# Sliding attention with a token-mixing MLP behind it: the first k heads loaded as fp32 by SyncE, the first GpSimd load held back, mixing by token halves, and a new order

## The chip, the cores and the metric

The kernel runs on 1 core of one Trainium2 chip. The metric is the device time of one execution, in microseconds (us). Engines are called as in the profile: PE is TensorE (its matmuls; PEld its weight loads), ACT is ScalarE, DVE is VectorE, POOL is GpSimd, SP is SyncE. SP does no arithmetic here: it issues DMAs (transfers), as POOL does beside some small work of its own. PE writes into PSUM, eight banks that the kernel uses as four pairs; only ACT and DVE carry results out of PSUM.

## The reference

Eight batches, eight heads, 576 tokens, 64 columns per head. Attention looks back over a window of 128 tokens with a penalty linear in the distance; its output, heads side by side, is a 576 x 512 matrix per batch, which a small MLP then mixes over the tokens.

```python
scores = scale * np.matmul(q, k.transpose(0, 1, 3, 2))
mask = (rel >= 0) & (rel < window)
scores = np.where(mask, scores + bias[None], -1000000000.0)
attn = softmax(scores)
x = np.matmul(attn, v)              # heads side by side: (B, S, 512)

wq, wk = x @ w_q, x @ w_k           # 64 columns each
W_tok = scale * np.einsum('bsd,btd->bst', wq, wk)
mixed = np.einsum('bst,btd->bsd', W_tok, x)
out = np.maximum(mixed, 0.0) @ w_out
```

The softmax lines and the reshaping are shortened here. The mixing is computed as wq times (wk transposed times x), so no 576 x 576 matrix is formed for it.

## The kernel before

The whole program is one unrolled list of small steps. Each step has a name, runs on one engine, and is a handful of instructions. The text ORDER at the head of the file is the schedule: a list of words `name:engine:bank`, made beforehand by a search, and every engine works through its own words strictly in that order. Nothing is reordered on the chip; a step whose input is late holds up all that stands behind it on its engine.

The steps of batch b, by name:

- Lq, Lk, Lv b.n: loads of q, k, v, issued by POOL, which cast fp32 to fp16 on the way. For b below 4, Lq b.u and Lk b.u bring heads 4u to 4u+3 (into tiles natw). Lt are the last 64 tokens (natt). Lwq, Lwk, Lwo are the weights. A load waits until an earlier load has landed, so that few are under way at a time (AHEAD in `load`).
- FQ0 and FQ1: q's heads 0 to 3 of batch 0 come another way. SP loads two heads each as fp32 into spare output tiles (osb), and CQ0 and CQ1 cast them on ACT or DVE into natw (`add_first`, cast in line 230 or 232).
- TW (or TN from batch 4 on, TT for the last 64 tokens): transposes of q and k on PE; ETW, ETN, ETT: their copies from PSUM into qkT.
- QK b.g.u: scores of key group g for four heads; EXP b.g.u: the exponential on ACT into pt; MUL b.g.u: times a table (bias, or biasl for the last group) on DVE, which also zeroes what lies outside the window. 64 of each.
- PV b.t: attention times v, with the row sum; X b.t: division by it on DVE (lines 654 and 655).
- XT, EXT: transposes of x and their copies. WQ b.0 and b.1 (256 tokens each) and b.2 (64 tokens), EWQ: the projection with w_q. WK, EWK: that with w_k. G, EG: wk transposed times x.
- MX b.j: the mixing matmul. For j = 0 and 1 it makes two of the four blocks of 128 columns for tokens 0 to 511, so it needs both EWQ b.0 and EWQ b.1; j = 2 is for the last 64 tokens. RM: the ReLU from PSUM into rm, one tile per block of 128 columns.
- OUT b.s: the output matmul for 128 tokens, four matmuls that add up over the four blocks of rm, so it needs RM b.0 to b.3. EO: its copy out of PSUM. DO: the store, issued by SP or POOL.

What is prepared at the start: iota (POOL), dist, mask (the table's distances, far and wm, on DVE), bias0 and bias1 (eight exponentials of wm on ACT, line 303), biasl (DVE), and constant fills: ones, zeros, zerop, pads. A word like `TW0.0.0:P:00:14` also asks for 14 matmuls on constant data (tile fill) ahead of the step, which keep PE at work while it has nothing to do.

Of the kernel before, what the change touches and what calls it, by code (L numbers as in the profile page):

```python
# [13 lines left out]
P = 128  # L14
# [13 lines left out]
TOK = 4  # L28
PTW = 1088
# [8 lines left out]
FQ1:S ones0:V FQ0:S Lk0.0:G pads:V iota:G Lk0.1:G dist:V Lt0.0:G idh:V perm:V Lq0.1:G mask:V  # L38
Lt0.2:G ones2:V bias0:A Lt0.3:G zerop:V Lt0.1:G CQ1:V CQ0:A Lk1.1:G bias1:A TW0.0.0:P:00:14
Lv0.1:G TW0.0.1:P:01 ETW0.0.0:A biasl1:V Lq1.1:G ETW0.0.1:A biasl0:V Lv0.0:G QK0.0.0:P:1:5  # L40
QK0.2.0:P:2 EXP0.0.0:A ones4:G TW0.1:P:0:2 EXP0.2.0:A MUL0.0.0:V Lk1.0:G QK0.1.0:P:3
ETW0.1.0:V ETW0.1.1:A Lq1.0:G EXP0.1.0:A zeros:V QK0.1.1:P:0 QK0.0.1:P:1 ones3:V QK0.2.1:P:2
EXP0.1.1:A TT0:P:3 MUL0.2.0:V MUL0.1.0:V EXP0.2.1:A Lv0.2:G ETT0:V MUL0.1.1:V EXP0.0.1:A
QK0.3.0:P:0:3 QK0.3.1:P:2 Lv0.3:G EXP0.3.1:A MUL0.0.1:V Lwq:G TW1.1:P:1:2 EXP0.3.0:A Lv0.4:G
MUL0.3.1:V Lq2.1:G MUL0.2.1:V ETT1:A PV0.0:P:2 ETW1.1.1:A PV0.1:P:0 MUL0.3.0:V Lk2.1:G
ETW1.1.0:A X0.0:V ones1:G QK1.0.1:P:3:2 QK1.1.1:P:1 EXP1.0.1:A X0.1:V Lq2.0:G TW1.0:P:2:2
EXP1.1.1:A MUL1.0.1:V Lwk:G Lk2.0:G PV0.2:P:0 ETW1.0.1:A MUL1.1.1:V QK1.2.1:P:3 ETW1.0.0:A
Lv1.0:G X0.2:V PV0.3:P:1 EXP1.2.1:A QK1.0.0:P:2 Lv1.1:G wqq:V PV0.4:P:0 X0.3:V EXP1.0.0:A
QK1.2.0:P:3 Lv1.2:G X0.4:V EXP1.2.0:A XT0.0:P:1 QK1.3.0:P:2 MUL1.2.1:V XT0.1:P:0 EXT0.0:A
Lv1.3:G TW2.1:P:3 EXT0.1:V EXP1.3.0:A MUL1.0.0:V Lt1.2:G QK1.3.1:P:1 ETW2.1.1:A XT0.2:P:00  # L50
QK1.1.0:P:2 MUL1.2.0:V Lv1.4:G EXP1.3.1:A WQ0.1:P:01 EXT0.2:V WQ0.0:P:31 MUL1.3.0:V Lq3.0:G
WK0:P:00 EXP1.1.0:A EWQ0.1:V MUL1.3.1:V Lt1.3:G TW2.0:P:1 ETW2.1.0:A EWK0:V EWQ0.0:A Lk3.0:G
MUL1.1.0:V WQ0.2:P:01 PV1.0:P:2 ETW2.0.0:A QK2.0.1:P:3 EWQ0.2:V ETW2.0.1:A Lt1.0:G X1.0:V
PV1.1:P:0 EXP2.0.1:A QK2.0.0:P:1 Lt1.1:G X1.1:V PV1.2:P:2 EXP2.0.0:A QK2.2.0:P:3 Lwo.2:G
# [89 lines left out]
def kernel(  # L144
# [214 lines left out]


    loads = {}
    under, gate = [], []
    tw, tt, qkd, pvd = {}, {}, {}, {}

    def load(name, occ, serve, deps, emit, eng="POOL"):
# [23 lines left out]
    def add_first(i):  # L389
# [7 lines left out]
        def cast(o):  # L397
            cp(o.eng, natw_s[0][0][0][:, 2 * i:2 * i + 2, :], first)
# [531 lines left out]
```

## Time and profile before

| what | value |
|---|---|
| time, median of 3 runs | 138.32 us (138.3 to 139.66) |
| the profiled execution: its time | 138.74 us |
| its span (first to last instruction) | 137.0 us |
| PE busy | 125.1 us, 91% |
| ACT busy | 115.0 us, 84% |
| DVE busy | 114.0 us, 83% |
| POOL busy | 100.1 us, 73% |
| DMA traffic | 24.86 MB, mean 181 GB/s |

The profiled execution took 138.74 us, of which 137.0 us lie between its first and last instruction and 1.74 us around them. A line of the timeline gives the start, the duration, the engine, the line in the kernel, the operation and its tiles, and in square brackets how long the engine stood idle before it and which engine it waited for. The chain of waits is followed back from the last instruction, at each step to what released it. PE's busy time counts a matmul until its result is written, and matmuls overlap, so PE can be called busy and still have room.

### The profile page before, as it was taken

To read this page: it belongs to the slowest core of one execution; us is meant where nothing else is said; L and a number is where in the kernel's file an instruction comes from. 1 tells how busy PE (TensorE), PEld (TensorE's weight loads), DVE (VectorE), ACT (ScalarE), POOL (GpSimd) and SP (SyncE) were. 2 spreads that over 40 slices of the span, in tenths; PEclk is the share of its full clock that TensorE was granted. 3 is DMA by queue.
4 is the path that set the end of the run, shared out by engine and by line. 5 is a ranking of instruction groups with operands and counts; after the bars stand their busy time and mean duration, and the time that the engine had idled before them with its cause. 6 is when DMAs were issued, how large, how long until landed. Compare 5 with 4: busy or idle time off the path is not lost.

```text
span 137.0 us, 5557 instructions
## 1 busy us (share of the span) xinstructions
PE 125.1 (91%) x2366; PEld 82.0 (60%) x2366; DVE 114.0 (83%) x257; ACT 115.0 (84%) x190; POOL 100.1 (73%) x145
## 2 busy tenths in 40 slices
PE   6895799899999999999999999999998799999950
PEld 2344467686694766775676656666487665765410
DVE  6636898998899999999999999989999699983430
ACT  3687989999899899899999999889997699655720
POOL 6996999798999999999999999976880002340120
PEclk9999999999999999999999999999999999999996
DMA  4999999999999999999999999999999200899992
GB/s 129 152 157 177 186 171 197 179 160 179 190 164 166 156 155 156 153 149 148 141 135 149 143 142 149 284 164 242 285 359 150 20 0 5 330 319 361 359 313 84
DMA packets 92855, 24.86 MB, mean 181 GB/s; under 512 B 80256, under 2 KB 89344, under 8 KB 92832
## 3 DMA queue, kind: packets, MB, share of 16 engines
q0 software_dynamic: 89376, 18.88, 149.0%
q1 hardware_dynamic: 3456, 5.64, 12.0%
q8 instruction: 18, 0.29, 0.8%
q14 instruction: 5, 0.04, 0.1%
HBM read 29.62 MB, written 9.44 MB: 285 GB/s over the span
## 4 chain that ended last, share of the span: by engine, by line
PE 62%; issue 11%; DVE 10%; ACT 5%; DMA 5%; POOL 4%; POOLq 0%; DVEq 0%; ACTq 0%
PE pair L215 51%; PE pair L218 11%; DMA natw<-in_q_dram 5%; DVE x L655 4%; ACT pt L609 3%; POOL out_dram L224 2%; DVE pt L616 2%; DVE xtl L655 2%; DVE inv L654 1%; POOL natw L221 1%; ACT qkT L236 1%; DVE qkT L499 1%; POOL natt L221 1%; DVE wqq_sb L344 0%; ACT natw L230 0%
## 5 line engine op out<-in xcount | busy, mean ns | idle before, releaser
L609 ACT ACTIVATE pt<-pair 128x1024 f16<-128x1024 f32 x64 | 63.7, 1037 | 4.7 <-PE pair L215 4.3
L221 POOL DMA_DIRECT2D vt<-in_v_dram x40 | 35.6, 927 | 3.3 <-DMA natw<-in_k_dram 2.3
L616 DVE TENSOR_TENSOR pt<-pt,bias 128x1024 f16<-128x1024 f16 x48 | 32.1, 684 | 2.5 <-ACT pt L609 2.1
L215 PE MATMUL pair<-wout_sb,rm 128*128 128x512 f16 x128 | 32.0, 380 | 0.1
L224 POOL DMA_DIRECT2D out_dram<-natw x17 | 10.0, 594 | 22.5 <-DVE natw L232 18.9
L215 PE MATMUL pair<-qkT 64*128 64x256 f16 (+3 forms) x352 | 23.7, 243 | 2.5 <-issue 1.1
L215 PEld LDWEIGHTS <-pt 128*128 128x128 f16 x576 | 20.3, 97 | 5.8 <-issue 3.2
L215 PE MATMUL pair<-vt,pt 128*128 128x65 f16 x576 | 23.4, 193 | 0.1
L221 POOL DMA_DIRECT2D natw<-in_k_dram x24 | 22.1, 938 | 1.4 <-POOLq L914 0.8
L655 DVE TENSOR_TENSOR x<-pair,inv 128x512 f16<-128x512 f32 x32 | 22.1, 691 | 1.1
L221 POOL DMA_DIRECT2D natw<-in_q_dram x23 | 21.4, 938 | 0.0
L215 PEld LDWEIGHTS <-rm 128*128 128x128 f16 x128 | 10.6, 97 | 12.4 <-issue 2.8
L215 PEld LDWEIGHTS <-qkT 64*128 64x128 f16 x352 | 11.3, 94 | 10.4 <-issue 5.5
L230 ACT COPY natw<-pair 128x512 f32<-128x512 f32 x23 | 13.8, 609 | 2.7 <-PE pair L215 2.4
L218 PEld LDWEIGHTS <-natw 128*64 128x64 f16 (+1 forms) x512 | 12.7, 102 | 4.2 <-issue 1.5
L215 PE MATMUL pair<-fill 128*128 128x512 f16 x30 | 9.3, 446 | 2.0 <-DVE fill L346 1.2
L755 ACT ACTIVATE rm<-pair 128x512 f16<-128x512 f32 x19 | 11.0, 617 | 0.0
L616 DVE TENSOR_TENSOR pt<-pt,biasl 128x1024 f16<-128x1024 f16 x16 | 10.8, 682 | 0.2 <-ACT pt L609 0.2
L218 PE MATMUL pair<-permh,natw 128*64 128x128 f16 x256 | 8.7, 221 | 1.4 <-DMA natw<-in_q_dram 0.8
L654 DVE RECIPROCAL inv<-pair 128x8 f32<-128x8 f32 (+1 forms) x40 | 8.1, 202 | 1.1 <-PE pair L215 0.8
L215 PE MATMUL pair<-xT,wqq_sb 128*128 128x256 f16 x64 | 8.8, 273 | 0.0
L757 DVE TENSOR_SCALAR rm<-pair 128x512 f16<-128x512 f32 x13 | 8.6, 683 | 0.1
(78 smaller groups left out, 177.7 us busy)
## 6 DMA issues: line engine op xcount, KB each, us to landing
vt<-in_v_dram POOLq DMA_DIRECT2D x32, 128.0 KB, 6.1
out_dram<-natw SPq DMA_DIRECT2D x15, 256.0 KB, 4.4
out_dram<-natw POOLq DMA_DIRECT2D x13, 256.0 KB, 4.8
natw<-in_k_dram POOLq DMA_DIRECT2D x8, 256.0 KB, 6.3
natw<-in_k_dram POOLq DMA_DIRECT2D x16, 128.0 KB, 5.0
natw<-in_q_dram POOLq DMA_DIRECT2D x16, 128.0 KB, 5.6
natw<-in_q_dram POOLq DMA_DIRECT2D x7, 256.0 KB, 6.6
osb<-in_q_dram SPq DMA_DIRECT2D x2, 256.0 KB, 2.9
```

The lines of the kernel that those rows point to most:

```text
L215: hold(nc.tensor.matmul(*a, **k))
L218: hold(nc.tensor.transpose(*a))
L221: hold(nc.gpsimd.dma_start(**k))
L224: i = (nc.gpsimd if eng == "POOL" else nc.sync).dma_start(**k)
L230: hold(nc.scalar.copy(out_ap, in_ap))
L236: hold(nc.scalar.copy(out_ap.bitcast(FP32), in_ap.bitcast(FP32)))
L609: nc.scalar.activation(out=pt[:, 0:1024], in_=two(s.bank).rearrange("p e c -> p (e c)"), func=AF.Exp, scale=SCALE)
L616: nc.vector.tensor_tensor(out=pt[:, 0:1024], in0=pt[:, 0:1024], in1=bt, op=ALU.mult)
L654: nc.vector.reciprocal(out=inv[r], in_=pxv[r, :, :, 64])
L655: nc.vector.tensor_tensor(out=x[r].rearrange("p (g h d) -> p g h d", g=2, h=4), in0=pxv[r, :, :, 0:64], in1=inv[r].unsqueeze(3).broadcast_ ...
L755: hold(nc.scalar.activation(out=out_ap, in_=in_ap, func=AF.Relu, scale=WSCALE))
L757: hold(nc.vector.tensor_scalar(out=out_ap, in0=in_ap, scalar1=0.0, scalar2=WSCALE, op0=ALU.max, op1=ALU.mult))
```

## The change

Four edits go together.

First, k's heads 0 to 3 of batch 0 are no longer loaded by POOL with a cast (Lk0.0 is gone). SP loads them as fp32, two heads at a time, as FK0 and FK1, and CK0 and CK1 cast them on chip. SP thus issues four loads at the start, in the order FK1, FQ1, FQ0, FK0. The first transposes of heads 0, 1 and of heads 2, 3 (TW0.0.0 and TW0.0.1) each need one q cast and one k cast.

Second, POOL's first load waits until SP's first load has landed.

Third, MX b.0 and b.1 are no longer split by column blocks but by tokens: MX b.j makes all four blocks for tokens 256j to 256j+255, and needs EWQ b.j alone. It is four matmuls of 256 columns in place of two of 512. RM b.2r+j carries two column blocks of that token half, and OUT b.s needs the two RMs of its own half in place of all four.

Fourth, some of the planned durations are changed, and ORDER is solved anew, so nearly every step stands elsewhere.

```diff
-    rm_s = [[sb(f"rm{i}{c}", [P, DM], F16) for c in range(4)] for i in range(2)]
+    rm_s = [[sb(f"rm{i}{n}", [P, 4, 256], F16) for n in range(2)] for i in range(2)]
...
             emit(o)
             n = len(under)
             late = 0.0
+            if not n:
+
+                tc.add_manual_dep(held[0], firsts[0][0].name, LANDED, reason="behind the first load of all")
...
-    def add_first(i):
-        first = osb_s[-1 - i].rearrange("p (h c) -> p h c", h=2)
+    def add_first(j, i):
+        first = (osb_end if i + j == 2 else osb_s[-1 - i - 2 * j]).rearrange("p (h c) -> p h c", h=2)
+        nm = "QK"[j]
 
         def em(o):
-            nc.sync.dma_start(out=first, in_=q[0, 2 * i:2 * i + 2, 0:512, :].rearrange("h (p t) d -> p h (t d)", t=4))
+            hold(nc.sync.dma_start(
+                out=first,
+                in_=(q, k)[j][0, 2 * i:2 * i + 2, 0:512, :].rearrange("h (p t) d -> p h (t d)", t=4)))
+            firsts.append(o.insts or list(held))
...
-            ts = [add(f"TW0.0.{a}", pe(0.46), [loads[0, 0, 0, a], loads[0, 1, 0], perm],
+            ts = [add(f"TW0.0.{a}", pe(0.46), [loads[0, 0, 0, a], loads[0, 1, 0, a], perm],
...
-                for r in range(2):
-                    h = slice(64 * r, 64 * r + 64)
-                    mm(pm[:, r, :], g[h, P * j:P * j + P], w[h, 0:512], start=True, stop=True)
+                for d in range(2):
+                    for r in range(2):
+                        h = slice(64 * r, 64 * r + 64)
+                        mm(pm[:, r, 256 * d:256 * d + 256], g[h, P * d:P * d + P],
+                           w[h, 256 * j:256 * j + 256], start=True, stop=True)
...
-        need = [ewq[b, 0], ewq[b, 1]] if j < 2 else [ewq[b, 2]]
-        t = add(f"MX{b}.{j}", pe(0.226, 0.1) if j < 2 else pe(0.06, 0.12), [egs[b], *need], em, banks=2, mode=1)
+        t = add(f"MX{b}.{j}", pe(0.23, 0.1) if j < 2 else pe(0.06, 0.12), [egs[b], ewq[b, j]], em, banks=2, mode=1)
...
-                lt = rm_s[b % 2][db][:, P * st:P * st + P] if st < 4 else rmt_s[(b // 2) % 2][:, db, :]
+                lt = rm_s[b % 2][st // 2][:, db, P * (st % 2):P * (st % 2) + P] if st < 4 else rmt_s[(b // 2) % 2][:, db, :]
...
-        need += [erm[b, db] for db in range(4)] if st < 4 else [erm[b, 4], erm[b - 1, 4]]
+        need += [erm[b, 2 * r + st // 2] for r in range(2)] if st < 4 else [erm[b, 4], erm[b - 1, 4]]
...
-FQ1:S ones0:V FQ0:S Lk0.0:G pads:V iota:G Lk0.1:G dist:V Lt0.0:G idh:V perm:V Lq0.1:G mask:V
+FK1:S ones3:V FQ1:S iota:G ones2:G ones1:V FQ0:S FK0:S ones4:V idh:V zeros:V CK1:A perm:V
```

Three places show how the order moves. The first is POOL's beginning. Before, it starts with Lk0.0 (natw_85), and Lk0.1 (natw_86), Lq0.1 (natw_84) and loads of the last tokens (natt) follow; Lk1.1 is natw_90, Lq1.1 natw_88, Lv0.1 vt_120.

```order
L221 DMA natw_85<-in_k_dram 128x4x256
L288 ISA
L288 IOTA wint 128x256
L221 DMA natw_86<-in_k_dram 128x4x256
L221 DMA natt_115<-in_q_dram 64x8x64
L221 DMA natw_84<-in_q_dram 128x4x256
L221 DMA natt_115<-in_q_dram 64x8x64
L221 DMA natt_115<-in_k_dram 64x8x64 x2
L221 DMA natw_90<-in_k_dram 128x4x256
L221 DMA vt_120<-in_v_dram 128x8x64
L221 DMA natw_88<-in_q_dram 128x4x256
```

Now, after iota and one set of ones, it goes on with Lq0.1.

```order
L222 DMA natw_84<-in_q_dram 128x4x256
L222 DMA natw_86<-in_k_dram 128x4x256
L222 DMA natt_115<-in_q_dram 64x8x64 x2
L222 DMA natt_115<-in_k_dram 64x8x64 x2
L222 DMA natw_90<-in_k_dram 128x4x256
L222 DMA natw_88<-in_q_dram 128x4x256
L222 DMA vt_120<-in_v_dram 128x8x64
```

Lk0.0 is gone from the queue, Lq0.1 is the first load and carries the new wait, and Lq1.1 is the eighth load where it was the tenth.

The second place is ACT's beginning: casts into natw (natw_83 is q, natw_85 is k), the tables bias_73 and bias_74 (bias0 and bias1), copies ETW into qkT, and the first exponentials into pt. Before:

```order
L303 ACTIVATE bias_73<-wm 128x256 x4
L230 CAST natw_83<-osb_188 128x512
L303 ACTIVATE bias_74<-wm 128x256 x4
L497 COPY qkT_81<-pair_190 128x2x256 x2
L609 ACTIVATE pt_144<-pair_191 128x1024
L609 ACTIVATE pt_148<-pair_192 128x1024
L497 COPY qkT_81<-pair_190 128x2x256
L609 ACTIVATE pt_146<-pair_193 128x1024
```

Now:

```order
L231 CAST natw_85<-osb_end 128x512
L231 CAST natw_83<-osb_184 128x512
L304 ACTIVATE bias_74<-wm 128x256 x4
L231 CAST natw_85<-osb_182 128x512
L304 ACTIVATE bias_73<-wm 128x256 x4
L508 COPY qkT_81<-pair_186 128x2x256
L620 ACTIVATE pt_148<-pair_187 128x1024
L620 ACTIVATE pt_146<-pair_188 128x1024
L620 ACTIVATE pt_144<-pair_189 128x1024
L508 COPY qkT_81<-pair_186 128x2x256
```

Three casts stand ahead of the second table in place of one, one of the two first ETW copies has gone to DVE, and three exponentials come before the next ETW in place of two. On DVE, ahead of mask (which makes wm), three sets of ones and zeros now stand where one set of ones and pads stood; pads and zerop come later.

The third place is ACT around EXP7.0.0, the first exponential of the last batch (pt_150). wqT_171 is EWQ5.0 and then EWQ5.1, qkT_82 is ETN7.1.1 before and ETN7.0.1 now, and xTt_169 is EXT5.2. Before:

```order
L609 ACTIVATE pt_149<-pair_192 128x1024
L230 COPY natw_103<-pair_190 128x512
L230 COPY natw_105<-pair_190 128x512
L609 ACTIVATE pt_150<-pair_193 128x1024
L230 CAST wqT_171<-pair_190 128x256
L609 ACTIVATE pt_152<-pair_192 128x1024
L230 CAST wqT_171<-pair_190 128x256
L236 COPY qkT_82<-pair_192 128x4x128
L609 ACTIVATE pt_153<-pair_191 128x1024
```

Now:

```order
L237 COPY qkT_82<-pair_188 128x4x128
L620 ACTIVATE pt_144<-pair_187 128x1024
L620 ACTIVATE pt_147<-pair_188 128x1024
L237 COPY xTt_169<-pair_189 128x4x32
L231 CAST wqT_171<-pair_186 128x256
L231 COPY natw_105<-pair_186 128x512
L620 ACTIVATE pt_150<-pair_187 128x1024
L231 CAST wkn_173<-pair_189 128x320
L231 CAST wqT_171<-pair_189 128x256
L620 ACTIVATE pt_153<-pair_188 128x1024
```

EWQ5.0 now stands ahead of EXP7.0.0 instead of behind it. On PE, five steps that stood behind QK7.0.0 now stand ahead of it: TN7.1.1 (16 transposes), XT5.1 (16), XT5.2 (4), WQ5.0 (4 matmuls of 256 columns) and WQ4.2 (4 of 64); none has gone the other way. In the last batches, OUT5.1 stands directly behind WK6, ahead of MX5.1, and the last step of the list is still OUT7.3 with its store in two halves.

More of the change, by code (lines that the diff above doesn't have):

```diff
@@ L28 @@
 TOK = 4
+MXN = 4
 PTW = 1088
@@ L37 @@
 ORDER = """
-FQ1:S ones0:V FQ0:S Lk0.0:G pads:V iota:G Lk0.1:G dist:V Lt0.0:G idh:V perm:V Lq0.1:G mask:V
[L39 to L49, printed above, removed]
@@ L456, in add_weights @@
             wts.append(load(nm, 0.55, 0.55, [], em))
-        wts[0] = add("wqq", DVE(0.25), [wts[0]], mk_wqq)
+        wts[0] = add("wqq", DVE(0.63), [wts[0]], mk_wqq)
         for c in range(4):
```

191 lines of the change are left out of this document (103 added, 88 removed).

## The prediction

> **What bounds the kernel now.** I read the chain of waits first, because it says which stretch belongs to whom; then the busy times by stretch, then the timeline at both ends. The chain's rows:
>
> ```profile
> 4.02 6.73 DMA natw<-in_q_dram
> ...
> 10.79 1.10 PE pair L218 x32
> ...
> 108.59 9.22 PE pair L215 x126
> ...
> 133.06 0.56 POOLq L925
> ```
>
> The beginning hangs on POOL's third large load (Lq0.1, issued at 4.02, landed at 10.75), the end on PE and then on the last store. Between them the busy times have to say more (columns: PE, PEld, DVE, ACT, POOL, clock, DMA share, GB/s):
>
> ```profile
> 60.00:70.00 10.00, 9.95 (x204) 6.37 (x201) 9.64 (x20) 9.96 (x18) 10.00 (x13) 1.00 2.22 142
> 100.00:110.00 10.00, 8.87 (x220) 7.05 (x215) 8.43 (x18) 7.90 (x15) 2.25 (x3) 1.00 1.07 156
> ```
>
> In the middle PE, DVE and ACT are all full; ACT at 9.96 of 10 sets the pace there, so an order can win little. From 100 on ACT and DVE have holes. There are three places where the change can count: until about 20 us, the last batch from 100 us, and the pace between, which I take as ACT's work.
>
> **The beginning.**
>
> ```profile
> 0.74 0.95 SPq L393 DMA_DIRECT2D osb<-in_q_dram  x2
> 1.25 0.28 DVE L321 MEMSET vt<- 64x264 uint32 x1
> 1.28 0.89 POOL L221 DMA_DIRECT2D natw<-in_k_dram  x1 [0.83 <-POOLq L914]
> 1.80 0.55 DVE L338 MEMSET xtl<- 128x256 uint32 x2
> 2.65 0.29 DVE L296 TENSOR_SCALAR farb<-wint 128x256 int32<-128x256 int32 x1
> 4.67 1.34 ACT L303 ACTIVATE bias<-wm 128x256 f16<-128x256 f32 x4 [2.65 <-DVE wm L293]
> 5.91 0.60 ACT L230 CAST natw<-osb 128x512 f16<-128x512 f32 x1
> 7.66 1.04 ACT L497 COPY qkT<-pair 128x512 f32<-128x512 f32 x2
> 8.61 0.77 POOL L221 DMA_DIRECT2D natw<-in_q_dram  x1
> 9.23 1.94 ACT L609 ACTIVATE pt<-pair 128x1024 f16<-128x1024 f32 x2 [0.54 <-PE pair L215]
> 11.92 0.59 ACT L497 COPY qkT<-pair 128x512 f32<-128x512 f32 x1 [0.74 <-PE pair L218]
> 12.84 0.55 DVE L329 MEMSET qkT<- 128x256 uint32 x2 [0.22 <-DVE qkT L499]
> 13.60 4.69 ACT L609 ACTIVATE pt<-pair 128x1024 f16<-128x1024 f32 x5 [0.17 <-PE pair L215]
> 20.04 1.94 ACT L609 ACTIVATE pt<-pair 128x1024 f16<-128x1024 f32 x2 [0.50 <-PE pair L215]
> ```
>
> How long loads take to land, from queries of single issues (SP's two; POOL's issues at 1.28, 2.55 and 8.61), and the traffic of the first 16 us in 40 slices of 0.4 us:
>
> ```profile
> osb<-in_q_dram SPq DMA_DIRECT2D x2, 256.0 KB, 2.9
> natw<-in_k_dram POOLq DMA_DIRECT2D x1, 256.0 KB, 5.5
> natw<-in_k_dram POOLq DMA_DIRECT2D x1, 256.0 KB, 5.7
> natw<-in_q_dram POOLq DMA_DIRECT2D x1, 256.0 KB, 7.0
> GB/s 0 0 0 0 72 110 335 374 361 95 81 115 156 170 150 188 179 169 157 136 156 179 171 142 157 153 154 172 190 185 167 170 181 191 190 175 208 162 172 193
> ```
>
> *SP's four loads.* Two issues take 0.95, so the four end at 2.6. The first lands at 0.74 + 2.9 = 3.6. The next are bound by the traffic: 256 KB at the some 360 GB/s of the slices around 3 us are 0.7 each, so 4.3, 5.0 and 5.7, for FQ1, FQ0 and FK0. No store is queued behind them on SP at that time.
>
> The Trainium skill ("DMA: Bandwidth & Descriptors", section "Issuing engines are not separate DMA queues") says that transfers of every issuing engine run on the same 16 DMA engines, and that issuing from several saves issue time only. That speaks against the first edit: k's bytes gain no bandwidth from SP's queue. The rows here show another price, 2.9 against 5.5 to land, and the second edit keeps the queues apart until 3.6; by the rule alone the k heads would land no sooner than before and the first score 1 us later, at the bound that the second rival takes from rows.
>
> *The table wm.* Three sets of ones and zeros stand ahead of it now, each 0.55 (from 1.25 to 1.80, and 0.55 for zeros), 2.2 in all, where ones and pads took 1.4 (1.25 to 2.65). So wm comes 0.8 later and ACT's first table starts at 5.5 instead of 4.67. ACT's casts CK1 (3.6 to 4.2) and CQ0 (5.0 to 5.6) fill its wait, and the second pushes the table to 5.6. From there two tables, one cast, as before: 4.67 to 7.66 was 3.0, so ETW0.0.1 at 8.6, and it is one copy, where two took 1.04. Scores begin after it at 9.2 instead of 8.7; the first exponential at 9.7 instead of 9.23.
>
> *The next wait.* ACT stood idle 0.74 before ETW0.1.1 at 11.92, and PE waited for Lq0.1. That load is now POOL's first, issued at 3.6: landed at 9.1 (by 5.5) to 10.3 (by the 6.73 that Lq0.1 took). Lk0.1 comes one issue later (0.77), at 10.1 to 11.1. TW0.1 takes 1.10, so it is done between 11.2 and 12.2. The three exponentials run from 9.7 to 12.6 (0.95 apart, 1.94 for two and 4.69 for five), so ACT no longer waits there. It then makes ETW0.1.1 (0.6), waits some 0.5 for scores as at 20.04, and goes on at 13.7, level with 13.60. Up to the ninth exponential one more ETW copy is on DVE (0.5 of ACT) and the wait of 0.50 at 20.04 has other work ahead of it: 19.2 instead of 20.04.
>
> *What stands behind POOL's wait.* All other loads. Lq1.1 is the eighth: 3.6 and seven issues of 0.77 is 9.0, plus 7.0 lands at 16.0, where it was 8.61 + 7.0 = 15.6. TW1.1 could start on PE at about 15.1, once its bank pair is read, so up to 0.9 of the gain goes to this wait. The beginning is worth -0.8 to +0.2; I take -0.3, nearer to the end with the wait.
>
> **The middle.** Small copies change engines.
>
> ```profile
> L230 ACT CAST wqT<-pair 128x256 f16<-128x256 f32 x14 | 5.3, 392 | 0.3 <-PE pair L215 0.2
> L215 PE MATMUL pair<-wqT,gs 64*128 64x512 f16 x32 | 5.2, 379 | 0.0
> L215 PE MATMUL pair<-x,wkn 128*64 128x256 f16 x64 | 5.0, 278 | 0.0
> ```
>
> Up to EXP7.0.0 ACT has six instructions more than before, two of them CK0 and CK1, which lie in its wait at the start (uncovered they would cost 0.6 each). The other four are small ones; at 0.39 (the half-size cast) at most 1.6, at least nothing, since larger ones went to DVE in exchange. I take +0.6. Splitting the mixing costs PE nothing: 32 matmuls of 512 columns took 5.2, and 64 of 256 columns (the row of wkn) 5.0. ReLU tiles keep their size, 512 columns each.
>
> **The last batch.**
>
> ```profile
> 100.44 1.14 ACT L609 ACTIVATE pt<-pair 128x1024 f16<-128x1024 f32 x1
> ...
> 105.47 0.28 PE L215 MATMUL pair<-qkT 64*128 64x256 f16 x1
> ...
> 106.87 0.38 PE L215 MATMUL pair<-qkT 64*128 64x256 f16 x3 [1.12 <-issue]
> ...
> 128.30 3.62 PE L215 MATMUL pair<-wout_sb,rm 128*128 128x512 f16 x16
> ```
>
> EXP7.0.0 starts at 100.44, and PE ends 31.5 later, at 131.92. From there PE is the bound with few holes; the one hole of 1.12 lies inside a step of four matmuls and no semaphore explains it. The new order has five PE steps fewer to do behind QK7.0.0. Their prices:
>
> ```profile
> L215 PE MATMUL pair<-xT,wqq_sb 128*128 128x256 f16 x64 | 8.8, 273 | 0.0
> L218 PE MATMUL pair<-identh,x 64*128 64x64 f16 x256 | 7.1, 195 | 0.6 <-DVE x L655 0.5
> L218 PE MATMUL pair<-identh,natw 64*128 64x64 f16 x256 | 6.4, 190 | 0.0
> L215 PE MATMUL pair<-xTt,wqq_sb 128*128 128x64 f16 x32 | 2.3, 194 | 0.0
> ```
>
> WQ5.0 is 4 of 64: 0.55. XT5.1 is 16 of 256: 0.44. TN7.1.1 16 of 256: 0.40. WQ4.2 4 of 32: 0.29. With XT5.2, a quarter of XT5.1, 1.8 together. A matmul's mean (0.273 in the first row) is longer than its share of the busy time (8.8 / 64 = 0.138), so about 0.14 of each step is only the tail of its last matmul, and the five are worth at least 1.1; but if PE must now squeeze them in ahead of QK7.0.0 where ACT needs scores, nothing is won at all. I take -1.4: PE has room where ACT sets the pace.
>
> Token halves let OUT5.1 and MX b.0 start earlier, so PE has more ready work between late copies. At the very end OUT7.0 waits for two ReLUs in place of four; but the last 16 matmuls took 3.62 without a gap (0.226 each), with two other OUTs ahead of them, so that wait was covered already and the last OUTs gain nothing. For holes before that, 0 to -1.5; I take -0.2. From PE's end to the span's end (5.1: copy, store, landing) nothing changes.
>
> Sum: -0.3 + 0.6 - 1.4 - 0.2 = -1.3 on the span of 137.0, so 135.7, and with the 1.74 around it 137.4 against 138.74 profiled. The median of the runs is 0.42 below the profiled one: **137.0**. Its own range is 135.9 to 138.2.
>
> **Rivals.**
>
> *The end shrinks more.* If earlier OUTs and the halves fill PE's holes behind 100 us, and the unexplained 1.12 falls where PE is not the bound, the last term is -2.0 instead of -0.2: 135.2. For it: ACT's 7.90 and DVE's 8.43 in that stretch. Against: 31.5 us hold mostly work. The Trainium skill ("Runtime: NRT & Kernel Launch", section "Instruction fetch mechanics") says that PE's instructions come in blocks of 256 through their own queue, mostly hidden. If the hole is such a block coming late, it comes back at the same count of instructions, and no order removes it; the row shows only that no engine was waited for.
>
> *POOL's late start is not caught up.* This one is slower. POOL's first load starts at 3.6 instead of 1.28, 2.4 later; one load less gives back 1.4 (1.28 + 5.5 against 2.55 + 5.7 landed). So the loads for batch 1, Lq1.1 for TW1.1 and Lk1.0 for TW1.0, come 1.0 later where the queue is served one after the other, 2.4 where a load's time is its own; the middle, 1.7, goes into the first exponentials of batch 1 and is never regained, since ACT is full from there. If the squeeze also eats the -1.4, it gives 138.3 + 1.7 = 140.0. It decides from Lq1.1 landing after about 16.9, later than my 16.0 by one exponential. Against: seven loads in place of nine stand ahead of Lq1.1.
>
> *Nothing stays.* ACT's pace rules from 20 to 115, so PE's earlier steps delay scores as much as they save: 138.3.
>
> **Chances.** Forecast 0.50, end shrinks more 0.17, POOL late 0.20, nothing stays 0.13. One per cent, about what this kernel's measurement can tell from no change, is 1.4, so 136.9 parts faster from same and lies in the forecast's own range: of its 0.50, 0.24 are faster and 0.26 same. Faster 0.24 + 0.17 = 0.41; same 0.26 + 0.13 = 0.39; slower 0.20. The range goes from 134.9, just past the first rival, to 139.9, leaving out the slower half of POOL's and some of the first's tail.
>
> **What will show it.** In the changed profile: casts from osb at 3.6 and 5.0; the first exponential at 9.7 (below 9.2, and my reading of wm is wrong; above 10.5, and SP's loads landed late); POOL's first load issued at 3.6; the ninth exponential at or before 20; EXP7.0.0 between 100.5 and 101.5, and PE's end no more than 30.3 behind it. If TW1.1 waits for natw beyond 16.9, the second rival holds. If EXP7.0.0 comes after 102.5, ACT's list or PE's squeeze was underrated and the sum is wrong in the middle.

## The result: 0.9 per cent slower, and the profile after

| what | before | after |
|---|---|---|
| median of 20 runs each | 138.16 us | 138.94 us |
| ratio, after to before | | 1.0091, 95% interval 1.0068 to 1.0114 |
| profiled execution: span | 137.0 us | 138.2 us |
| the 17th exponential (the first of batch 2) | 31.8 | 32.5 |
| EXP7.0.0 (the 57th) | 100.4 | 103.7 |
| PE's end | 131.92 | 132.14 |
| from PE's end to the span's end | 5.1 | 6.1 |

The forecast was 137.0 us and a gain; by the ratio the kernel became some 1.2 us slower, while the medians of all runs differ by 0.8. Executions of one kernel spread by 2 to 3%; the ratio leaves out those more than 1.5% above the fastest, and both profiled ones are among these (138.74 and 139.98 in all), so what they show is set at the end of this section beside undisturbed profiles, those of experiments whose execution the ratio counts. The timeline of after, at the places that the prediction named (start, duration, engine, line, operation, idle time before it and its releaser):

```profile
3.68 0.62 ACT L231 CAST natw<-osb_end 128x512 f16<-128x512 f32 x1 [1.66 <-DMA osb_end<-in_k_dram]
3.96 0.92 POOL L222 DMA_DIRECT2D natw<-in_q_dram  x1 [1.86 <-DMA osb_end<-in_k_dram]
5.97 0.62 ACT L231 CAST natw<-osb 128x512 f16<-128x512 f32 x1 [1.67 <-DMA osb<-in_q_dram]
9.07 0.82 POOL L222 DMA_DIRECT2D natw<-in_q_dram  x1
10.42 2.85 ACT L620 ACTIVATE pt<-pair 128x1024 f16<-128x1024 f32 x3 [0.39 <-PE pair L216]
17.29 1.08 PE L219 MATMUL pair<-permh,natw 128*64 128x128 f16 x32 [1.46 <-DMA natw<-in_q_dram]
20.14 2.88 ACT L620 ACTIVATE pt<-pair 128x1024 f16<-128x1024 f32 x3
103.71 1.06 ACT L620 ACTIVATE pt<-pair 128x1024 f16<-128x1024 f32 x1
128.52 3.62 PE L216 MATMUL pair<-wout_sb,rm 128*128 128x512 f16 x16
```

The first cast comes at 3.7, as forecast. The next cast on ACT waits for FQ0 until 5.97 instead of 5.0, and the first exponential starts at 10.42 instead of 9.7. Lq1.1, issued at 9.07, holds PE up until 17.29, and the ninth exponential (the second in the row at 20.14) starts at 21.1. EXP7.0.0 is 3.3 later than before, but PE ends only 0.2 later.

The chain of waits of after (start, duration, what) says the same of the beginning, and ends on POOL's last store as before:

```profile
0.74 2.92 DMA osb_end<-in_k_dram
...
9.07 8.17 DMA natw<-in_q_dram
...
17.29 1.10 PE pair L219 x32
...
133.28 0.56 POOLq L939
```

How long single loads took to land in after: SP's first (FK1), SP's third (FQ0), and POOL's Lq1.1:

```profile
osb_end<-in_k_dram SPq DMA_DIRECT2D x1, 256.0 KB, 2.9
osb<-in_q_dram SPq DMA_DIRECT2D x1, 256.0 KB, 4.2
natw<-in_q_dram POOLq DMA_DIRECT2D x1, 256.0 KB, 8.2
```

The stretch from about the 17th exponential to PE's end, cut at EXP7.0.0. First before, then after (columns: stretch, length, busy time of PE, PEld, DVE, ACT and POOL, clock, DMA share, GB/s):

```profile
31.80:100.44 68.64, 68.14 (x1403) 45.72 (x1401) 65.66 (x129) 65.58 (x106) 65.24 (x83) 1.00 2.09 176
100.44:131.92 31.48, 30.35 (x482) 19.06 (x478) 23.37 (x46) 22.94 (x45) 6.73 (x12) 1.00 0.80 208
```

```profile
32.50:103.71 71.21, 70.79 (x1477) 48.60 (x1476) 67.94 (x134) 66.52 (x109) 64.98 (x81) 1.00 2.11 166
103.71:132.14 28.43, 28.11 (x442) 17.95 (x438) 21.30 (x42) 21.74 (x42) 5.40 (x10) 1.00 0.69 236
```

Up to EXP7.0.0 PE does 74 matmuls more than before and the stretch is 2.57 longer; behind it PE does 40 fewer and the stretch is 3.05 shorter. (Of the 34 more in all, 32 come from the token halves, which need four matmuls where two did.) The two stretches together are 100.12 before and 99.64 after. And PE's busy time fills both: 98.49 of 100.12 before, 98.90 of 99.64 after.

Last, the microseconds behind PE's end, before and after in the same columns:

```profile
131.92:132.92 1.00, 0.00 (x0) 0.00 (x0) 0.42 (x1) 0.37 (x1) 0.00 (x0) 1.00 0.97 373
132.92:133.92 1.00, 0.00 (x0) 0.00 (x0) 0.00 (x0) 0.00 (x0) 0.54 (x1) 1.00 0.97 355
133.92:134.92 1.00, 0.00 (x0) 0.00 (x0) 0.00 (x0) 0.00 (x0) 0.00 (x0) 0.69 0.48 165
134.92:135.92 1.00, 0.00 (x0) 0.00 (x0) 0.00 (x0) 0.00 (x0) 0.00 (x0) 0.50 0.00 0
```

```profile
132.14:133.14 1.00, 0.00 (x0) 0.00 (x0) 0.42 (x1) 0.37 (x1) 0.00 (x0) 1.00 0.99 369
133.14:134.14 1.00, 0.00 (x0) 0.00 (x0) 0.00 (x0) 0.00 (x0) 0.54 (x1) 1.00 1.02 382
134.14:135.14 1.00, 0.00 (x0) 0.00 (x0) 0.00 (x0) 0.00 (x0) 0.00 (x0) 0.94 0.84 298
135.14:136.14 1.00, 0.00 (x0) 0.00 (x0) 0.00 (x0) 0.00 (x0) 0.00 (x0) 0.50 0.07 23
```

GB/s over 1 us is KB: 373 + 355 + 165 = 893 KB are written behind PE's end before, and 369 + 382 + 298 + 23 = 1072 KB after. In the first 2 us the DMA engines are full in both (shares of 0.97 to 1.02), so the extra 179 KB take time: some 0.5 us, an estimate at the 370 GB/s of these rows. The last store is issued at the same distance behind PE's end in both, 1.14 us (133.06 before, 133.28 after). It takes longer to land, first before, then after (the last column, us):

```profile
out_dram<-osb_end POOLq DMA_DIRECT2D x1, 128.0 KB, 2.0
out_dram<-osb_end POOLq DMA_DIRECT2D x1, 128.0 KB, 3.1
```

So the two profiled spans differ by +0.7 up to the 17th exponential, -0.48 from there to PE's end, and +0.98 behind it: +1.2. The undisturbed profiles of the experiments divide it otherwise (a kernel counts where the order of PE's steps in that stretch is the old or the new one; in the last line, where its end is unchanged too; the kernel with token halves alone, whose tail was 6.5, is left out there):

| stretch, us | forecast | these two profiles | old, undisturbed | new, undisturbed | difference |
|---|---|---|---|---|---|
| to the 17th exponential | -0.3 | +0.7 | 31.3 (five, 31.0 to 32.1) | 31.4 (six, 31.1 to 31.8) | +0.1 |
| from there to PE's end | +0.6 - 1.4 - 0.2 | -0.48 | 99.5 (six, 98.9 to 100.0) | 99.7 (six, 99.6 to 99.8) | +0.2 |
| behind PE's end | 0 | +0.98 | 5.0 (three, 4.8 to 5.1) | 5.8 (five, 5.5 to 6.0) | +0.8 |

Together +1.1, close to what the ratio gives. The first two lines lie within the spread of the old profiles; the third does not. The rest lies outside the span, where the forecast took 1.74 for both kernels: in the 135 runs of before that accompany the experiments this time is 1.73 to 1.87 (mean 1.79), in the 20 of after 1.73 to 2.50 (mean 1.92).

### The profile page after: what moved, and what is told of

It reads as the page before. It is cut to its first block, busy times and chain, and to the rows that moved or that the text cites. A ratio compares the mean times of both kernels' runs of the same rounds, so it can differ in the third digit from the quotient of the medians.

```text
span 138.2 us, 5646 instructions
## 1 busy us (share of the span) xinstructions
PE 126.3 (91%) x2400; PEld 84.1 (61%) x2400; DVE 114.8 (83%) x264; ACT 114.8 (83%) x191; POOL 96.2 (70%) x134
## 4 chain that ended last, share of the span: by engine, by line
PE 59%; ACT 10%; DMA 8%; issue 7%; DVE 7%; POOL 5%; POOLq 0%; DVEq 0%; ACTq 0%
PE pair L216 48%; PE pair L219 10%; ACT pt L620 6%; DMA natw<-in_q_dram 6%; DVE pt L627 2%; DMA osb_end<-in_k_dram 2%; POOL natt L222 2%; DVE x L666 2%; POOL out_dram L225 2%; POOL natw L222 2%; ACT qkT L237 1%; ACT qkT L508 1%; ACT natw L231 1%; DVE inv L665 1%; DVE xtl L666 1%
## 5 line engine op out<-in xcount | busy, mean ns | idle before, releaser
L222 POOL DMA_DIRECT2D vt<-in_v_dram x40 | 37.4, 993 | 3.2 <-DMA natw<-in_q_dram 2.7
L225 POOL DMA_DIRECT2D out_dram<-natw x14 | 8.9, 675 | 26.0 <-ACT natw L231 22.4
L222 POOL DMA_DIRECT2D natw<-in_q_dram x23 | 21.9, 974 | 2.4 <-DMA osb_end<-in_k_dram 1.9
L216 PE MATMUL pair<-qkT 64*128 64x256 f16 (+3 forms) x352 | 23.1, 243 | 0.1
L766 ACT ACTIVATE rm<-pair 128x512 f16<-128x512 f32 x20 | 11.7, 612 | 0.2 <-PE pair L216 0.2
L216 PE MATMUL pair<-fill 128*128 128x512 f16 x32 | 9.8, 456 | 1.6 <-DVE fill L347 1.2
L216 PE MATMUL pair<-xT,wqq_sb 128*128 128x256 f16 x64 | 9.5, 274 | 0.0
L239 DVE COPY xT<-pair 128x1024 f16<-128x1024 f16 x10 | 6.9, 687 | 1.8 <-PE pair L219 0.9
```

The costliest lines, as they stand in the source:

```text
L216: hold(nc.tensor.matmul(*a, **k))
L222: hold(nc.gpsimd.dma_start(**k))
L225: i = (nc.gpsimd if eng == "POOL" else nc.sync).dma_start(**k)
L239: hold(nc.vector.tensor_copy(out=out_ap, in_=in_ap))
L766: hold(nc.scalar.activation(out=out_ap, in_=in_ap, func=AF.Relu, scale=WSCALE))
```

## The experiments

All ratios are to the kernel before, run beside it on the same chip, with 95% intervals. "PE's end from the 17th" is the time from the 17th exponential to PE's end; "tail" is from PE's end to the span's end.

### Which of the edits costs the time

**The old beginning with the new order behind it.** The old loads, casts and words up to QK2.0.1, then the words of after, and the mixing by token halves.

```diff
-FK1:S ones3:V FQ1:S iota:G ones2:G ones1:V FQ0:S FK0:S ones4:V idh:V zeros:V CK1:A perm:V
+FQ1:S ones0:V FQ0:S Lk0.0:G pads:V iota:G Lk0.1:G dist:V Lt0.0:G idh:V perm:V Lq0.1:G mask:V
```

> The beginning of the kernel before (up to the first score unit of batch 2, loads by POOL as before) and from there the new order with mixing by token halves. Theory 'beginning' (the late start of POOL's loads costs about 1 us at the ninth exponential, and the rest of the new order is better than the old): the ninth exponential at about 20.0 as before, PE's end about 1 us earlier than the changed kernel's 132.1, and a ratio to before of 0.992 to 0.998. Rival 'end' (the lost microsecond lies behind PE's end, where the last stores land 1 us later): PE's end at or below 131.9 but the span still 6 us behind it, and a ratio of 1.003 to 1.010.

Measured: 1.0131 (1.0069 to 1.0192), above what either theory gave. Its profiled execution had a lower granted clock (mean 0.976, against 0.988 in after's), so its own stretches are not read here. The old beginning does not rescue the new order.

**The new beginning with the old order behind it.** The reverse, with mixing by column blocks.

```diff
+FK1:S ones3:V FQ1:S iota:G ones2:G ones1:V FQ0:S FK0:S ones4:V idh:V zeros:V CK1:A perm:V
-FQ1:S ones0:V FQ0:S Lk0.0:G pads:V iota:G Lk0.1:G dist:V Lt0.0:G idh:V perm:V Lq0.1:G mask:V
```

> The beginning of the changed kernel (k by SP, the wait, the new order up to the first score unit of batch 2) and from there the old order with mixing by column blocks. Theory 'beginning': the delay of 1 us at the ninth exponential is carried to the end, since the old rest makes up nothing: ratio 1.008 to 1.016, span 5.1 behind PE's end. Rival 'end': ACT and PE take up the delay before the last batch, and with the old stores the ratio is 0.998 to 1.004.

Measured: 1.0025 (0.9985 to 1.0066), first exponential at 10.5, ninth at 19.8, tail 5.0. The new beginning costs little or nothing, and with it the ninth exponential can be on time. The windows of this kernel, in the columns of those above:

```profile
31.80:100.63 68.83, 68.21 (x1402) 45.73 (x1400) 65.50 (x129) 65.72 (x105) 64.89 (x83) 1.00 2.08 173
100.63:131.27 30.64, 30.36 (x483) 19.13 (x478) 23.39 (x46) 23.13 (x45) 8.23 (x13) 1.00 0.88 223
```

With the old order, PE is busy for 98.57 of 99.47 here. The 1.12 hole of before is not there, and what is left free on PE is 0.9.

**Token halves alone.** The kernel before with the new mixing, nothing else.

```diff
-                    mm(pm[:, r, :], g[h, P * j:P * j + P], w[h, 0:512], start=True, stop=True)
+                        mm(pm[:, r, 256 * d:256 * d + 256], g[h, P * d:P * d + P],
+                           w[h, 256 * j:256 * j + 256], start=True, stop=True)
```

> The kernel before with only the mixing by token halves, in the old order. The forecast priced the split at nothing on PE: ratio 0.998 to 1.002, and the last OUTs unchanged since their ReLUs were covered. Rival: twice as many weight loads and matmuls in MX cost PE 0.1 us a step, 16 steps, 1.6 us: ratio 1.008 to 1.012.

Measured: 0.9999 (0.9958 to 1.004). By form, its mixing matmuls cost PE what the 32 of 512 columns cost before (5.2):

```profile
L215 PE MATMUL pair<-wqT,gs 64*128 64x256 f16 x64 | 5.2, 270 | 0.0
```

So the halves neither cost nor win. This run's tail is 6.5; the section on the tail comes back to it.

**After without POOL's wait.**

```diff
-            if not n:
-
-                tc.add_manual_dep(held[0], firsts[0][0].name, LANDED, reason="behind the first load of all")
```

> The changed kernel without the wait of POOL's first load. Theory 'the wait delays batch 1': Lq0.1 is issued at about 2.2, Lq1.1 lands 1 to 1.7 earlier than 17.25, the ninth exponential comes at 19.5 to 20.3 instead of 21.1, and if that counts at the end the ratio to before is 1.000 to 1.004 in place of 1.009. Rival 'SP's loads suffer': without the wait both queues share the DMA engines, FQ0 and FK0 land 0.5 to 1.5 later, the first exponential comes at 11 to 12, and the ratio stays at 1.008 to 1.015.

Measured: 1.0107 (1.0054 to 1.016). FQ0 and FK0 land 0.8 and 1.8 later than in after and the first exponential starts at 11.2, as the rival said; the ninth comes at 20.5 in place of 21.1, and the ratio does not fall. The wait is not the cost.

**A mended beginning.** After, with what wm needs first on DVE, and Lk1.1 and Lq1.1 ahead of the loads of the last tokens.

```diff
+idh:V perm:V dist:V mask:V
 ones1:V
...
+Lk1.1:G Lq1.1:G
 Lt0.0:G
```

> The changed kernel with idh, perm, dist and mask ahead of the second and third set of ones on DVE, and Lk1.1 and Lq1.1 ahead of the four last-token loads on POOL. Theory 'the beginning costs': the first exponential comes at 9.6 to 10 instead of 10.42, Lq1.1 lands near 15.5 instead of 17.25, the ninth exponential comes at 19.5 to 20.3, and the ratio to before is 1.000 to 1.004. Rival 'the beginning is absorbed': the ninth exponential is as early, and the ratio stays at 1.007 to 1.011.

Measured: 1.0098 (1.0062 to 1.0134), the first exponential at 10.5 as in the other kernels with this beginning: ACT waits for FQ0 first, so an earlier table wins nothing. The ninth comes at 20.2, as early as the theory asked, and the ratio stays, as the rival said.

The five results put the cost into the new order behind QK2.0.1, not into the wait or the halves; the new beginning may have a quarter of it (1.0025) or nothing.

### The steps drawn ahead of QK7.0.0

**QK7.0.0 earlier again.** After, with QK7.0.0 ahead of OUT4.3, WQ5.0, WQ4.2 and XT5.2, and its exponential right behind EXP6.2.1.

```diff
-QK6.2.1:P:2 OUT4.3:P:00 WQ5.0:P:01 WQ4.2:P:30 XT5.2:P:31 QK7.0.0:P:1
+QK6.2.1:P:2 QK7.0.0:P:1 OUT4.3:P:00 WQ5.0:P:01 WQ4.2:P:30 XT5.2:P:31
-EWQ5.0:A EO4.3:A EXP7.0.0:A
+EXP7.0.0:A EWQ5.0:A EO4.3:A
```

(PE's and ACT's words alone are shown.)

> The kernel after, with QK7.0.0 ahead of OUT4.3, WQ5.0, WQ4.2 and XT5.2 on PE, and its exponential EXP7.0.0 right behind EXP6.2.1 on ACT: it gives back three of the five steps that the change drew ahead. Theory 'a step drawn ahead costs the scores behind it what it saves later': EXP7.0.0 starts 1 to 1.8 us earlier than the 103.7 of after, PE's end stays at 99.3 to 100.0 us behind the 17th exponential, ratio 1.007-1.011. Theory of the forecast (PE has room ahead of QK7.0.0, and only the order behind decides): EXP7.0.0 moves by less than 0.5 us and PE's end goes back by 0.7 to 1.5 us, ratio 1.012-1.018.

```profile
31.62:101.41 69.79, 68.76 (x1436) 46.91 (x1435) 66.58 (x131) 65.49 (x106) 65.14 (x81) 1.00 2.12 161
101.41:132.08 30.67, 30.35 (x477) 19.77 (x475) 22.73 (x45) 22.85 (x45) 5.41 (x10) 1.00 0.73 240
```

Measured: 1.0167 (1.012 to 1.0214). EXP7.0.0 starts 69.8 behind the 17th exponential where it was 71.2 in after, 1.4 earlier; behind it 2.2 come back (30.67 against 28.43), so PE's end is 0.8 later. EXP7.0.0 moved as the first theory said, PE's end and the ratio as the forecast's did: having the four steps ahead cost 1.4 and saved 2.2. One of the four is OUT4.3, which stood ahead of QK7.0.0 before the change too, so these are not the prices of the drawn steps alone. Yet with that won, after's order stands only level with the old one at PE's end.

### The tail

**Ready stores early.** In both orders nine stores whose data are long ready stand behind others that wait, and the DMA engines then have next to nothing to move, for some 10 us from 106.5 on in before and some 5 us from 108.5 on in after. They were put ahead: in after, in before, and in before with token halves. First after's words, then those of before:

```diff
+DO1.4:S DO4.0:S DO0.1:S DO1.2:S DO1.1:S DO2.1:S
 DO5.1:S
...
+DO2.3:G DO1.0:G DO4.2:G
 DO5.2:G
```

```diff
+DO1.1:S DO3.3:S DO0.0:S DO4.2:S DO2.1:S
 DO5.1:S
...
+DO0.1:G DO3.4:G DO4.3:G DO1.0:G
 DO5.2:G
```

> The changed kernel with nine stores of outputs that are long ready (six on SP, three on POOL) put ahead of the first store that waits in the last batch (DO5.1, DO5.2), so that the DMA engines work in the gap after 107 us. Theory 'stores' (the changed kernel loses its microsecond behind PE's end, because its last stores stand in a backlog): span 5.0 to 5.2 behind PE's end in place of 6.1, ratio to before 0.998 to 1.003 in place of 1.009. Rival 'rest' (the new order's exponentials from batch 2 on are slower): ratio stays at 1.007 to 1.011.

> The kernel before with nine ready stores put ahead of DO5.1 and DO5.2 in the same way. Theory 'stores': before ends 5.1 behind PE's end and its last store lands 2.0 after its issue, so it has almost no backlog to lose: ratio 0.996 to 1.000. Rival: the old kernel's end is bound by the stores as well, and the ratio is 0.985 to 0.992.

> The kernel before, with mixing by token halves and the nine stores put ahead. With the halves alone PE ended at 129.9, 2.0 earlier than before, but the span ended 6.5 behind it. Theory 'stores': the halves do speed up the last batch and the stores' backlog hides it: ratio 0.982 to 0.992. Rival: PE's early end in that one profile was the luck of a hole that PE did not have (1.1) and a quiet clock, and the ratio is 0.996 to 1.001.

Measured: 1.0083 (1.0049 to 1.0117), 0.99 (0.9814 to 0.9985, from two of its six runs), and 1.0036 (0.9989 to 1.0083). The tails are 5.8, 5.0 and 5.1: no backlog of stores makes the new one longer. The second kernel was run again:

> The kernel s2_old_stores_early once more, since its ratio of 0.99 came from two runs alone. If stores that go out early save time by themselves, 0.988-0.995, and this beats both kernels. If what remains behind PE's end decides, and the kernel before leaves only 0.88 MB there, nothing is won: 0.997-1.003.

Measured: 0.9954 (0.9909 to 0.9998), tail 5.0, PE's end 100.0 from the 17th. It is the one version that may beat both kernels, by half a per cent, at the edge of what 12 runs tell. By the medians of all runs the gain is less sure still: 138.97 against 138.24 the first time, 137.81 against 138.05 the second. No row of its profile shows where the gain would come from.

**A shorter program for SP, and the last stores on two queues.** By then a sixth packet on the queue that the profile calls "q14 instruction" had been seen near the end of the kernels with the new order, where the old ones have five. In after, DO3.4 and DO1.4 go to POOL; then DO7.0 too. In before, five early stores go from POOL to SP.

```diff
-DO3.4:S
...
-DO1.4:S
...
+DO3.4:G DO1.4:G DO5.2:G
```

> The kernel after, with the stores DO3.4 and DO1.4 moved from SP to POOL just ahead of DO5.2, which takes four instructions off SP's program (28 rows for 32). Theory 'the program's length': in every kernel so far that ends 5.5 us or more behind PE's end on a full-length SP program (32 rows) a sixth packet of instructions (q14) moves in the last 6 us and shares a DMA engine with the last stores; with the shorter program it is gone, the span ends 5.0 to 5.3 us behind PE's end, and the ratio falls from 1.008-1.010 to 1.001-1.005. Rival 'the last stores stand on one queue': DO7.0, 7.2, 7.1 and 7.3.0 still all leave through SP, so the span ends 5.5 to 6.1 us behind PE's end and the ratio stays 1.007-1.011.

```diff
-DO7.0:S
+DO7.0:G
```

> The same with DO7.0 on POOL too, as in the kernel before (SP 27 rows). Theory 'the program's length': no further change, ratio within 0.2% of p1_new_short_sp. Rival 'the last stores stand on one queue': only here does the end fall to 5.0 to 5.2 us behind PE's end, and the ratio to 1.002-1.005.

```diff
-DO3.4:G DO0.1:G DO4.3:G DO1.0:G DO1.4:G
+DO3.4:S DO0.1:S DO4.3:S DO1.0:S DO1.4:S
```

> The kernel before, with the early stores DO3.4, DO0.1, DO4.3, DO1.0 and DO1.4 issued by SP rather than POOL (SP 33 rows), its last stores as they were. Theory 'the program's length': a sixth q14 packet appears in the last 8 us, the span ends 5.6 to 6.1 us behind PE's end, ratio 1.004-1.008. Rival 'the last stores stand on one queue': 5.0 to 5.2 us behind PE's end, ratio 0.998-1.002.

Measured: 1.0073 (1.0039 to 1.0108) with a tail of 5.9; 1.008 (1.0046 to 1.0114) with 6.0; 1.0028 (0.999 to 1.0065) with 4.8. The sixth packet stayed in the first two and did not come in the third. Both theories fell: neither SP's program nor its share of the last stores makes the tail.

**The last burst of stores.** What does differ is when the last store ahead of batch 7's five goes out. Before, DO6.0 leaves on SP 3.56 ahead of PE's end. In after its counterpart DO6.3 waits on POOL for a copy that stands one step further back on DVE:

```profile
129.26 0.54 POOL L225 DMA_DIRECT2D out_dram<-natw  x1 [3.61 <-DVE natw L233]
```

That is 2.88 ahead of PE's end. The first edit takes this out of after: RM7.1 on ACT, so that EO6.3 comes sooner, and DO6.3 on SP. The second puts it into before.

```diff
-RM7.1:V EO6.3:V OUT7.0:P:01 EO7.4:A DO6.3:G
+RM7.1:A EO6.3:V OUT7.0:P:01 EO7.4:A DO6.3:S
```

> The kernel after, with one of its last mixed copies, RM7.1, on ACT instead of DVE, so that DVE comes to the copy EO6.3 one step sooner, and with that copy's store DO6.3 on SP instead of POOL. Theory 'the last burst of stores starts late': the kernel after leaves 1.04 to 1.09 MB to be written behind PE's end, where the kernels with the old order leave 0.88 to 0.92 MB, because its last store ahead of batch 7's five goes out 2.88 us ahead of PE's end and not 3.56; with the edit it goes out 3.4 us ahead of it or earlier, 0.88 to 0.95 MB are left, the span ends 5.0 to 5.3 us behind PE's end, and the ratio falls to 1.002-1.006. Rival 'a late packet of instructions holds one DMA engine': the sixth q14 packet stays in the last 6 us, so the span still ends 5.5 to 6.1 us behind PE's end, ratio 1.007-1.010.

```diff
-RM7.1:A RM7.0:V
+RM7.0:V RM7.1:V
...
-DO6.0:S EO7.4:A
+EO7.4:A DO6.0:G
```

> The kernel before, with its last burst made late in the same way: RM7.1 on DVE instead of ACT ahead of the copy EO6.0, and the store DO6.0 on POOL instead of SP. Theory 'the last burst of stores starts late': DO6.0 goes out 2.7 to 2.9 us ahead of PE's end rather than 3.56, 1.0 to 1.1 MB are left behind it, the span ends 5.4 to 5.9 us behind PE's end, ratio 1.003-1.007. Rival 'a late packet of instructions': five q14 packets, none late, and the span ends 4.8 to 5.1 us behind PE's end, ratio 0.998-1.002.

The mended end, in the windows behind PE's end, and DO6.3's issue (the first of three in a row of SP's timeline):

```profile
127.19 1.88 SPq L225 DMA_DIRECT2D out_dram<-natw  x3
```

```profile
130.75:131.75 1.00, 0.00 (x0) 0.00 (x0) 0.42 (x1) 0.37 (x1) 0.00 (x0) 1.00 0.95 352
131.75:132.75 1.00, 0.00 (x0) 0.00 (x0) 0.00 (x0) 0.00 (x0) 0.54 (x1) 1.00 1.00 364
132.75:133.75 1.00, 0.00 (x0) 0.00 (x0) 0.00 (x0) 0.00 (x0) 0.00 (x0) 1.00 0.53 190
133.75:134.75 1.00, 0.00 (x0) 0.00 (x0) 0.00 (x0) 0.00 (x0) 0.00 (x0) 1.00 0.01 4
```

Measured for the mended end: DO6.3 goes out 3.56 ahead of PE's end, 910 KB are left, tail 5.45, ratio 1.0037 (0.9996 to 1.0077). Bytes and ratio came out as expected, the tail fell only part of the way. For the late end in before: 1019 KB are left, the tail grows to 5.3, and the ratio is 0.9998 (0.9955 to 1.0042), where 1.003 to 1.007 was expected. Bytes moved as the theory says, in both directions; the time followed only in one.

**Stores early and the mended end together**, both edits as above.

> The kernel s1_new_stores_early (after, with nine stores that are long ready ahead of those that wait) with the mended end of v1_new_end_mended as well. If a backlog of stores and the late burst both count: the span ends 4.8 to 5.0 us behind PE's end, ratio 0.999-1.003. If the burst alone counts: as v1_new_end_mended within 0.2%. If neither: 5.5 us or more, 1.007-1.010.

Measured: 1.0058 (1.0012 to 1.0104), 927 KB, tail 5.5: within its interval the same as the mended end alone.

**The packet, put into the old order.** A count of each engine's program, waits that stand alone among them, put the kernels on DVE at 328 instructions where the sixth packet comes and at 319 or fewer where it does not. (The rows of the profiles are some four fewer, 324 or 325 against 303 to 315. The sorting is not clean: PE too has at least two matmuls more in the first group, and in the kernel with the old beginning and the new order a sixth packet does come, 1.8 us behind the span's end.) So 21 one-column fills were added on DVE to before, and to before with the late end.

```diff
+        if name in ("EO6.3", "EO7.1"):
+            for c in range(8) if name == "EO6.3" else range(8, 21):
+                nc.vector.memset(spare[:, c:c + 1], 0.0)
         op.emit(op)
```

> The kernel before, with 21 one-column fills of a spare tile added on DVE, in two holes of its last 10 us (eight ahead of EO6.3, thirteen ahead of EO7.1), so that DVE's program is as long as that of after. Every kernel with the sixth q14 packet has a DVE program of 328 instructions, counting waits that stand alone, and every one without it 319 or fewer; no other engine's program sorts them so. Theory 'a late packet of instructions holds one DMA engine': the sixth packet comes within 1 us of PE's end and is gone from nothing else; about 0.88 MB are left behind PE's end as before, and the span ends 5.3 to 5.6 us behind it, ratio 1.001-1.005. Rival 'only the burst counts': 4.8 to 5.1 us, ratio 0.998-1.002.

> The kernel v2_old_end_late with the same 21 fills on DVE: late burst and late packet in the old order. If the two add up, some 1.02 MB are left behind PE's end, and the span ends 5.6 to 6.0 us behind it, as in after, ratio 1.003-1.007. If the packet does nothing, 5.2 to 5.3 us, ratio 0.999-1.003.

Packets, MB and share in the DMA view: of before, of the first of these kernels over its span, and of that kernel's 1 us from 127.0.

```profile
q14 instruction: 5, 0.04, 0.1%
```

```profile
q14 instruction: 6, 0.05, 0.2%
...
q14 instruction: 1, 0.01, 4.2%
```

The sixth packet came, in both: it belongs to DVE's program. But it came some 3 us ahead of PE's end, not within 1 us of it. It held a DMA engine for 0.67 us in the first (4.2% of 16 engines in 1 us) and 0.31 in the second. Tails 5.6 and 5.1, ratios 0.9998 (0.9962 to 1.0035) and 0.9996 (0.9955 to 1.0037). So at that place it costs nothing that the runs show.

All profiled tails, sorted by the two suspects:

| kernels | KB left behind PE's end | late instruction packet | tail, us |
|---|---|---|---|
| before and five with the old end | 876 to 910 | none | 4.8 to 5.1 |
| old end, DVE's program longer | 942 | 3.2 ahead of PE's end | 5.6 |
| late end in the old order, two kernels | 1019, 1020 | none; 2.7 ahead | 5.3, 5.1 |
| new order: old beginning (the profile with the lower clock); mended beginning | 1035, 1100 | none; 2.3 ahead | 5.5, 5.5 |
| new order, end mended, two kernels | 910, 927 | at PE's end, both | 5.45, 5.5 |
| after and five more of the new order | 1042 to 1084 | 0.2 to 0.6 behind PE's end | 5.7 to 6.1 |
| token halves alone | 904 | q8, 2 to 3 behind PE's end | 6.5 |

Against 5.0 with the old end, some 120 to 200 KB more go with 0.1 to 0.5, a packet at PE's end with some 0.45, both with 0.8 to 1.1. These are single executions; the second row and the last, with tails of 5.6 and 6.5 at 942 and 904 KB, show that bytes alone do not set the tail. In the timed runs only the removal of the late burst shows, and its interval touches that of after.

## Why the prediction was wrong, point by point

- **The tail, "nothing changes": wrong. The sum has it at nothing; the runs show +0.8, most of what the kernel lost.** The new order's tail is 5.5 to 6.1 where kernels with the old end have 4.8 to 5.1. The last copy and the last store do come at the same distance behind PE's end, as the forecast had it; the landing does not (3.1 after the issue against 2.0), since the forecast did not look at what else the DMA engines have to write then. One large RM7 copy more on DVE and one store on POOL instead of SP push 256 KB 0.7 later, into a stretch where the engines are full. That this sets the time is shown from one side only: undoing it took the ratio from 1.0091 to 1.0037, with intervals that touch, and putting it into the old order cost nothing in the timed runs.
- **"PE has room where ACT sets the pace": wrong, and with it -1.4 and the halves' -0.2. By the busy times, this is why no gain came.** From the 17th exponential to PE's end -1.0 was forecast, and the undisturbed profiles show +0.2, the largest miss of the sum. The window from 60 to 70 showed PE at 9.95 and ACT at 9.96; the forecast took the second as the limit. From the 17th exponential on PE is busy for 98.3 to 99.1 us in either order (the profile with the lower clock aside), ACT for 88 to 89, so by these rows an order can win little more than PE's idle time: 1.6 in the profile of before, 0.9 in the kernel with the new beginning and the old order. Of the -1.0, -0.48 shows in the two profiles and nothing in the undisturbed ones. The price of the drawn steps was not absurd: undoing three of them, with OUT4.3, cost 0.8. But the stretch up to EXP7.0.0 gave back 2.6 where +0.6 was allowed.
- **EXP7.0.0 "between 100.5 and 101.5": 103.7.** In the undisturbed profiles of the new order it is 102.3 to 103.6. The stated sign (after 102.5, the middle is wrong) was the right one. PE's end "no more than 30.3 behind it" came true, 28.4, and told nothing alone.
- **The beginning: -0.3, measured +0.7 in this profile, +0.1 in the undisturbed ones.** The wait of POOL and the first cast were read rightly. FQ0 was not: the sum let the four loads follow one another at 360 GB/s and land at 5.0 for FQ0; it lands at 5.9, 4.2 after its issue, although POOL issues nothing before 3.96. ACT's first table waits behind its cast, so the first exponential starts at 10.4. That the ninth is late too happens only where Lq1.1 lands late: 8.2 in this execution, 5.7 to 7.4 in seven others with the same issues, where TW1.1 started between 15.5 and 16.6.
- **The rivals.** "POOL's late start is not caught up" named the side of the result, and its sign (TW1.1 waiting beyond 16.9) stands in this profile, but not in the undisturbed ones, and without the wait the ratio stays 1.0107: it was right about the side by luck. For the same reason it says little that the median, 138.94, lies within the forecast's 134.9 to 139.9, whose upper part was there for this rival. "Nothing stays" describes the stretch up to PE's end. "The end shrinks more" did not come, and no rival had the tail. The unexplained hole of 1.12 does come back at the same count, behind PE's 2013th matmul, in seven more profiles that keep the old order there, as 0.2 to 1.2 us; a q8 packet started 1.2 to 1.5 us ahead of the long holes and 1.8 to 2.2 ahead of those under 0.5. That speaks for instructions that come late. The profiles of the new order have no hole there, so it is not fixed for every order, and of before's 31.5 us about 1 was such a draw.
- **Token halves cost PE nothing: right,** 5.2 against 5.2 in the kernel that has them alone. What the sum left out is that PE's program grows by 32 matmuls and as many weight loads, which may be what lengthens the time outside the span (next paragraph).

What stays open: with its end mended the new order is still 0.4 to 0.6% behind. In the runs that the ratio of the mended end counts, the span is 0.25 us longer than before's, and the time outside the span is 2.12 in the mean of all runs against 1.79. Six profiles, all of kernels with token halves, have a q8 packet that ends 1.9 to 3.2 us behind the span's end, and in these the time outside the span is 1.89 to 3.00, longer the later the packet ends; in the others it is 1.76 to 2.03. So part of what is missing is probably a packet of instructions that the execution still waits for. The new beginning (1.0025, its interval holds 1) and a packet at PE's end are candidates for the rest; a kernel of the new order with a shorter DVE program was not tried. Nor is it settled why a late end costs nothing in the old order.

## What to carry to other kernels

Where two engines are both recorded as full, add their busy times over the whole stretch that the change touches before calling one of them the pace: here no order won more than the idle time of the fuller one. Count the bytes that are still to be written behind the last matmul, and look at how long the last store takes to land, not only at when it is issued: here a copy and a store that slipped left 0.1 to 0.2 MB more there. Keep the time outside the span as a row of its own. And a single profile of a beginning with queued loads is one draw: the same load landed after 5.7 to 8.2 us.

## What the runs showed of the hardware

- Packets of instructions share the DMA engines with the data. In after the sixth q14 packet lies 0.6 behind PE's end, and one of the 0.25 us windows there reads:

```profile
q14 instruction: 1, 0.01, 7.7%
```

7.7% of 16 engines in 0.25 us is 0.31 us of one engine. A q8 packet takes longer; in the kernel with token halves alone one falls between 132 and 133, behind PE's end at 129.92:

```profile
q8 instruction: 1, 0.02, 5.5%
```

That is 0.88 us of one engine, and this kernel's last stores landed 3.4 to 3.9 after their issue, against 2.0 and 2.1 in before, with about as many bytes left (904 and 893 KB). That the packet is the cause is argued from the place, not shown.
- The number of q14 packets within the span went from five to six when DVE's program was made longer by 21 instructions; the fills took 0.38 us in all and lay in DVE's idle time.
- Casts by ACT from a tile that SP loads start right where the load lands (3.68 for a landing at 3.66), so in this kernel the loads set the beginning and not the casts.
